# Four pairs of PSUM banks for a convolution, whole-batch-pair Fourier sums, and convolution units joined without emptying the array

## The chip, the cores and the metric

One NeuronCore of a Trainium2 chip runs the kernel. The metric is device time in microseconds of one execution. Everything below is about one core; TensorE is called PE, VectorE DVE, ScalarE ACT, GpSimd POOL and SyncE SP, as in the profile.

## The reference

A causal convolution over 3264 positions with 7 softmaxed taps per head (8 heads of 24 channels), then a Fourier layer: the first 64 modes of each channel are mixed by a 192 x 192 complex matrix per mode, transformed back and added to the signal, and a ReLU branch is added.

```python
# x: (8, 3264, 192), weight: (8, 7)
w = softmax(weight)                                  # per head
x = einsum('hk,bskhg->bshg', w, windows_of_7(x))     # causal, zero-padded
X = rfft(x, axis=1)[:, :64]
Yr = Xr @ w_r - Xi @ w_i                             # per mode, 192 x 192
Yi = Xr @ w_i + Xi @ w_r
u = x + irfft(Y, n=3264)
out = u + maximum(u @ w_ch, 0)
```

## The kernel before

The whole signal is held on chip in `xall`, in bf16: two batches at a time form a pair `q` (3 to 0, in the order in which they are loaded), and a pair's positions are six blocks `b` (5 to 0) of 256 rows in each half of the sequence, and a rest. POOL issues all loads of x (line 194) in that order, then those of the mixing weights (line 329). The weights of the first eight groups of four modes go to places in `ct` that are empty then, those of the next four to `arena`, which the convolution's stage also uses, and the rest to `arena` again as groups are done. All engines run in the order in which the program text issues their instructions.

**Convolution.** The blocks are cut into six *units* (the list at line 57: pair, first block, number of blocks, whether the rest rows belong to it). For each unit, `conv_head` (line 369) is called for 8 heads. A head is four steps: two output banks `a` by two inputs `b`. A step has lower matmuls (array rows 0 to 63) and upper ones (rows 64 to 127), which accumulate into the same bank. The upper matmuls of a step are put off by three steps (`LAG`, line 356, the list `upper`), so that both halves of the array work; `flush()` (line 359, called at line 546 after each unit) issues what is still put off. After a head's last upper step two instructions, one for each bank, carry the result from PSUM back to `xall` as bf16 (lines 403 and 405), on DVE for heads 0, 4 and 7 (0 and 7 where three folds fall into the unit), on ACT for the others. The banks come from `next_banks` (line 334): a ring of seven. The eighth bank, `sums[0]`, accumulates the Fourier sums. `rows_ahead` (line 338) copies edge rows of a pair from the top block to the rest, at the start of the unit that holds the top block.

**Fourier sums.** `fold` (line 417) makes sum and difference of the two halves of a piece of a unit, on DVE, in one of three places of `arena` in turn; it is called after heads 1 and 5 (1, 3 and 5) for the pieces of the unit before. After the unit's `flush()`, `xtrans` (line 451) transposes the sums of a pair that is done, and `dft` (line 427) multiplies the folded pieces with the table, 64 columns wide for each of two halves. The last unit's pieces are not folded: their products take the whole array, with twice the passes.

**Transposed copies.** 42 *jobs* (`tjobs`, line 511) transpose `xall` and the tables into `ct` and `gtab`, a bank of up to eight 128 x 128 transposes and a copy on DVE or ACT each. Six are done after the first unit, four after the third (lines 555 to 557), the others between the convolution and the mix (line 523, `trans_banks`) and in the mix.

**Mix and output.** The loop at line 918 goes over 16 groups: `mix(g)` (12 products with the weights, line 586), one or two jobs, products that are made ahead, and from group 1 on the transposition of the results (line 614). After group 13 all jobs that are left are done (line 946). `keep_busy` (line 904) issues products whose result isn't used. The output stage (line 832, a planned order) does the transformation back, ReLU, the additions and the stores.

Of the kernel before, what the change touches and what calls it, by code (L numbers as in the profile page):

```python
# [19 lines left out]
def kernel(  # L20
# [37 lines left out]
             [(1, 4, 2, 0), (1, 2, 2, 0), (1, 1, 1, 0)], [(1, 0, 1, 1), (0, 4, 2, 0), (0, 3, 1, 0)],  # L58
             [(0, 1, 2, 0), (0, 0, 1, 1)]]
# [77 lines left out]
    def temp(n, dtype):  # L137
# [23 lines left out]
    sides = [arena[:, FB * i:FB * (i + 1)].rearrange("p (r b t i d) -> p r b t i d", r=2, b=2, t=2, i=2)  # L161
             for i in (2, 1, 0)]
    assert pos[0] <= NWA * WGB - FB and NWA * WGB == 3 * FB
# [17 lines left out]
    cz = hand_out("left", "cv", (1, 1, 1, 1))  # L181
    sums = hand_out("right", "sum", (1, 1))
    stacks["sum"] = stacks.pop("right")
    cz += hand_out("right", "cv", (1, 1)) + [sums[1]]
# [149 lines left out]
    def next_banks():  # L334
        rot[0] += 2
        return [cz[(rot[0] - 2 + i) % 7] for i in range(2)]

    def rows_ahead(q):

        k = 2 + 4 * (NBH - 1)  # L340
        z = next_banks()
        for i in range(2):
            for h in range(2):
                nc.tensor.matmul(z[i][64 * (1 - h):64 * (1 - h) + 64, 0:2 * D], ahead[64:P, :],
                                 xall[64:P, q, k + 2 * h + i, :, :].rearrange("p t d -> p (t d)"), start=True,
                                 stop=True, tile_position=(64, 64 * (1 - h)), skip_group_check=True)
            engine = nc.vector.tensor_copy if i else nc.scalar.copy
            for h in range(2):
                r = slice(64 * (1 - h), 64 * (1 - h) + R0)
                engine(out=xall[r, q, i, :, :].rearrange("p t d -> p (t d)"), in_=z[i][r, 0:2 * D])  # L350
# [18 lines left out]
    def conv_head(u, h, engine):  # L369
        z = next_banks()  # L370
# [11 lines left out]
        def put(src, dst, c, a, b, fa, fb, back=0, start=False, stop=False):  # L382
# [3 lines left out]
            return nc.tensor.matmul(z[a][64 * dst:64 * dst + 64, GRP * (fa - f0):GRP * (fb - f0)],  # L386
# [3 lines left out]
        def later(a, b, name):  # L390
# [7 lines left out]
            if a == 1 and b == 0:  # L398
                for v in range(2):
                    dst = cflat[:, f0 // 2:f1 // 2, v, :, cols]  # L400
                    srcv = z[v][:, 0:GRP * (f1 - f0)].rearrange("p (n i e) -> p n i e", i=2, e=GRP)
                    if engine == "v":
                        nc.vector.tensor_copy(out=dst, in_=srcv)  # L403
                    else:
                        nc.scalar.copy(out=dst, in_=srcv)  # L405
# [11 lines left out]
    def fold(q, b0, nb, rest):  # L417

        side[0] += 1
        cpm = sides[(side[0] - 1) % 3]  # L420
# [6 lines left out]
    def dft(q, b0, nb, rest, cpm):  # L427
        xp = sums[0][:, 0:2 * D]
        ops = []
        for t in range(2 * b0, 2 * (b0 + nb)):  # L430
            b, a = divmod(t, 2)
            if cpm is None:
                ops.append((ftab[:, t, :], call[:, q, 1 + 2 * b, a, :, :], slice(0, P)))
                ops.append((fneg[:, t, :], call[:, q, 2 + 2 * b, a, :, :], slice(0, P)))
            else:
                for r in range(2):
                    ops.append((ftab[:, t, :], cpm[:, r, b - b0, a, :, :], slice(64 * r, 64 * r + 64)))
        if rest:
            for a in range(2):
                for r in range(1 if cpm is None else 2):  # L440
                    ops.append((ftab[:, 2 * NBH + a, :], call[:, q, 0, a, :, :],
                                slice(0, P) if cpm is None else slice(64 * r, 64 * r + 64)))
        top = b0 + nb == NBH
        for k, (f, mv, sl) in enumerate(ops):
            nc.tensor.matmul(xp[sl, :], f[:, sl], mv, start=(top and k < 2),  # L445
                             stop=(rest == 1 and k >= len(ops) - 2), tile_position=(0, sl.start),
                             skip_group_check=True)
        if rest:
            nc.scalar.copy(out=xs[q % 2][:], in_=xp.rearrange("p (i d) -> p i d", i=2))

    def xtrans(q):
        z = next_banks()
        for i in range(2):
            tp = z[i][:, 0:3 * P].rearrange("p (j c) -> p j c", j=3)
# [6 lines left out]
        for i in range(2):  # L461
            b = 2 * (NQ - 1 - q) + i
            dst = xt[:, :, b:2 * B:B, 0:MODES]
            srcv = z[i][:, 0:3 * P].rearrange("p (j c m) -> p j c m", j=3, c=2)
# [64 lines left out]
    prev = []  # L529
    pend = []  # L530
    todo = []
    for k, u in enumerate(units):
        for q, b0, nb, rest in u:
            if b0 + nb == NBH:
                rows_ahead(q)
        if k == 0:
            table(0)
        at = (1, 3, 5) if len(prev) == 3 else (1, 5)
        for h in range(H):
            conv_head(u, h, "v" if h in ((0, 7) if len(prev) == 3 else (0, 4, 7)) else "a")  # L540
            if h in at and prev:
                piece = prev.pop(0)
                todo.append((*piece, fold(*piece)))
            if k in (0, 1) and h == 6:
                table(k + 1)
        flush()
        for q in pend:
            xtrans(q)
        pend = []
        while todo and not pend:  # L550
            d = todo.pop(0)
            dft(*d)
            if d[3]:
                pend.append(d[0])
        if k in (0, 2):
# [428 lines left out]
```

## Time and profile before

| | us |
|---|---|
| Median of 3 runs | 176.45 (176.34 to 177.8) |
| The profiled execution | 175.09 |
| Its span, first to last instruction | 173.3 |
| First x that the chain of waits meets, landing | 26.84 |
| First product of the mix (line 586) | 78.36 |
| Line 586's last group | 107.9 |

The first 27 us are loads of x and the making of tables and taps, with the first unit. Units two to six, the sums and 16 of the jobs lie between 27 and 78, the mix between 78 and 108, and the output stage behind. A row of a view gives the start, the length, the engine, the line, what the instruction writes and reads, and in brackets the idle time before it and who ended it.

### The profile page before, as it was taken

Reading aid. Unit: us, or ns where it says so; the run is one execution under the profiler, and the core shown is the slowest. Engines: PE = TensorE matmul, PEld = TensorE weight load, DVE = VectorE, ACT = ScalarE, POOL = GpSimd, SP = SyncE. Lnnn points to the kernel's source line nnn. Section 1 sums busy time; section 2 is a strip of 40 time slices with the busy share of each in tenths; the row PEclk is TensorE's granted clock in tenths of the full one; section 3 lists DMA queues with packets and bytes.
Section 4 is the critical chain, followed back from the end, with each engine's and each line's share of the span. In section 5 each row is a group of like instructions: output and inputs, shape, how many; then the busy total and the mean of one; then the engine's idle time right before and its main releaser. Section 6 shows DMA issues by size and latency. Waiting matters only on the chain.

```text
span 173.3 us, 6286 instructions
## 1 busy us (share of the span) xinstructions
PE 152.2 (88%) x2635; PEld 116.2 (67%) x2635; DVE 133.0 (77%) x274; ACT 118.6 (68%) x250; POOL 64.3 (37%) x108
## 2 busy tenths in 40 slices
PE   0207988999999798998999999999999999999990
PEld 0004576666656565676776776688999988999960
DVE  3995589988997969735565653499998999999990
ACT  6736865557883836636767565588889899898860
POOL 7987969767766753082005500510000000000000
PEclk9999999999999999999999999999999999999997
DMA  3999999999999999999997994479879999999996
GB/s 29 179 183 199 201 202 200 202 201 203 201 201 196 203 208 205 206 207 206 207 179 110 194 193 82 103 269 362 315 253 371 395 352 356 351 354 392 377 351 197
DMA packets 38336, 40.72 MB, mean 235 GB/s; under 512 B 3652, under 2 KB 38212, under 8 KB 38308
## 3 DMA queue, kind: packets, MB, share of 16 engines
q0 software_dynamic: 23088, 19.96, 72.5%
q1 hardware_dynamic: 14948, 20.16, 32.4%
q8 instruction: 20, 0.33, 0.7%
q10 hardware_dynamic: 272, 0.20, 0.3%
q14 instruction: 8, 0.07, 0.1%
HBM read 39.43 MB, written 20.45 MB: 345 GB/s over the span
## 4 chain that ended last, share of the span: by engine, by line
PE 72%; DMA 9%; DVE 7%; POOL 6%; ACT 2%; issue 2%; POOLq 0%; DVEq 0%
PE outleft L733 18%; DMA xall<-in_x_dram 9%; PE sumright L733 9%; PE cvleft L386 8%; PE mixright L733 7%; PE trleft L504 7%; PE sumright L445 6%; POOL xall L194 5%; DVE arena L423 4%; PE cvright L386 3%; PE sumright L586 3%; PE trleft L733 2%; ACT ct L475 2%; PE mixright L614 2%; PE sumright L386 2%
## 5 line engine op out<-in xcount | busy, mean ns | idle before, releaser
L733 PEld LDWEIGHTS <-ct 64*128 64x128 bf16 x624 | 41.0, 94 | 5.0 <-PE trleft L733 0.5
L733 PE MATMUL outleft<-mixa,gtab 64*128 64x384 bf16 x182 | 41.9, 323 | 0.1
L386 PEld LDWEIGHTS <-band 64*64 64x64 bf16 x832 | 26.2, 108 | 23.0 <-issue 9.3
L386 PE MATMUL cvleft<-xall,band 64*64 64x432 bf16 (+7 forms) x484 | 34.6, 328 | 7.3 <-DMA xall<-in_x_dram 6.2
L194 POOL DMA_DIRECT2D xall<-in_x_dram x48 | 34.7, 735 | 8.5 <-DMA xall<-in_x_dram 7.2
L733 PEld LDWEIGHTS <-gtab 64*128 64x128 bf16 x416 | 30.9, 94 | 2.8 <-PE outleft L733 1.1
L779 ACT ACTIVATE outleft<-outleft 128x384 f32<-128x384 f32 x53 | 24.5, 477 | 4.6 <-PE outleft L733 2.3
L733 PE MATMUL mixright<-mixa,gtab 64*128 64x384 bf16 x90 | 25.8, 323 | 0.0
L733 PE MATMUL sumright<-mixa,gtab 64*128 64x384 bf16 x92 | 25.8, 323 | 0.0
L733 PE MATMUL outleft<-wb,ct 64*128 64x192 bf16 x104 | 23.1, 243 | 0.0
L386 PE MATMUL cvright<-xall,band 64*64 64x432 bf16 (+8 forms) x234 | 21.8, 329 | 1.3 <-DVE xall L403 0.8
L733 PE MATMUL outleft<-wa,ct 64*128 64x192 bf16 x104 | 22.9, 243 | 0.0
L733 PE MATMUL outleft<-wc,ct 64*128 64x192 bf16 x104 | 21.7, 243 | 0.0
L477 DVE COPY ct<-trleft 128x1024 bf16<-128x1024 bf16 (+1 forms) x18 | 11.8, 668 | 11.5 <-PE trleft L504 9.7
L405 ACT CAST xall<-cvleft 128x432 bf16<-128x432 f32 (+3 forms) x32 | 14.6, 519 | 8.5 <-DMA xall<-in_x_dram 3.5
L504 PEld LDWEIGHTS <-xall 128*128 128x128 bf16 x312 | 17.7, 98 | 3.7 <-issue 1.0
L423 DVE TENSOR_TENSOR arena<-xall 128x1536 bf16<-128x1536 bf16 (+1 forms) x24 | 19.2, 851 | 0.0
L801 DVE TENSOR_TENSOR arena<-outleft,xall 128x384 f32<-128x384 f32 x27 | 14.4, 554 | 2.5 <-PE outleft L733 2.1
L504 PE MATMUL trleft<-ident,xall 128*128 128x128 bf16 x234 | 16.2, 220 | 0.0
L403 DVE CAST xall<-cvleft 128x432 bf16<-128x432 f32 (+2 forms) x24 | 13.6, 603 | 3.1 <-PE sumright L386 2.0
L475 ACT COPY ct<-trleft 128x1024 bf16<-128x1024 bf16 x12 | 12.2, 1013 | 3.6 <-PE trleft L504 3.5
L386 PE MATMUL sumright<-xall,band 64*64 64x432 bf16 (+8 forms) x114 | 14.4, 324 | 0.0
(168 smaller groups left out, 339.3 us busy)
## 6 DMA issues: line engine op xcount, KB each, us to landing
xall<-in_x_dram POOLq DMA_DIRECT2D x48, 192.0 KB, 7.6
out_dram<-arena SPq DMA_DIRECT2D x23, 384.0 KB, 3.9
out_dram<-xall SPq DMA_DIRECT2D x13, 384.0 KB, 4.2
out_dram<-ct SPq DMA_DIRECT2D x8, 384.0 KB, 3.9
ct<-in_moe_w_r_dram POOLq DMA_DIRECT2D x8, 288.0 KB, 9.7
ct<-in_moe_w_i_dram POOLq DMA_DIRECT2D x8, 288.0 KB, 10.5
arena<-in_moe_w_r_dram POOLq DMA_DIRECT2D x8, 288.0 KB, 7.4
arena<-in_moe_w_i_dram POOLq DMA_DIRECT2D x8, 288.0 KB, 8.3
```

Source lines behind the costliest of these rows:

```text
L194: nc.gpsimd.dma_start(out=xall[:, q, k:k + 2, :, :].rearrange("p k t d -> p k (t d)"), in_=src)
L386: return nc.tensor.matmul(z[a][64 * dst:64 * dst + 64, GRP * (fa - f0):GRP * (fb - f0)], bd3[r, h, base:base + 64], xflat[r, fa - back:fb ...
L403: nc.vector.tensor_copy(out=dst, in_=srcv)
L405: nc.scalar.copy(out=dst, in_=srcv)
L423: nc.vector.tensor_tensor(out=cpm[:, r, 0:nb, :, :, :].rearrange("p b t i d -> p b (t i d)"), in0=src[:, :, 0, :], in1=src[:, :, 1, :], op=op)
L445: nc.tensor.matmul(xp[sl, :], f[:, sl], mv, start=(top and k < 2), stop=(rest == 1 and k >= len(ops) - 2), tile_position=(0, sl.start), sk ...
L475: nc.scalar.copy(out=out, in_=in_)
L477: nc.vector.tensor_copy(out=out, in_=in_)
L504: nc.tensor.transpose(o, cv.rearrange("p i d -> p (i d)")[:, P * blk:P * blk + P], ident[:])
L733: m = nc.tensor.matmul((Z[s % NZ] if bank is None else bank)[:, cols], l, r, start=start, stop=stop, skip_group_check=True)
L779: act = nc.scalar.activation(out=z, in_=z, func=ACT.Relu)
L801: add = nc.vector.tensor_tensor(out=o[:, :, a, :], in0=Z[s % NZ][:, 0:2 * D].rearrange("p (i d) -> p i d", i=2), in1=c_rows(q, kk)[:, a, : ...
```

## The change

All eight banks go to the convolution as four tiles of two banks. A head takes one tile (`next_pair`), and one instruction carries both banks out; DVE does heads 0 and 4 (0, 1, 3 and 5 of the first unit), ACT the others. `rows_ahead` uses one tile and two instructions of twice the length, and for the last two pairs is called after head 4 of the unit before. The units have four blocks each. Folds go to six places in turn, three in `arena` and three in `ct` of the second pair. `dft` is called once for a batch pair, with all its pieces, when its last piece has been folded, and accumulates in a tile of the same ring; `xtrans` of a pair comes just before the next pair's `dft`. `flush()` is called after the first and the last unit only, so that the put-off steps of the others run beneath the next unit's first head, behind whatever is issued between. After the third unit two jobs are done in place of four. The tables of `table(1)` and `table(2)` are made two units later. The mix takes four banks of its own, two of which first get a product each whose result isn't used.

```diff
     units = [[(3, 4, 2, 0), (3, 2, 2, 0)], [(3, 0, 2, 1), (2, 4, 2, 0)], [(2, 2, 2, 0), (2, 0, 2, 1)],
-             [(1, 4, 2, 0), (1, 2, 2, 0), (1, 1, 1, 0)], [(1, 0, 1, 1), (0, 4, 2, 0), (0, 3, 1, 0)],
-             [(0, 1, 2, 0), (0, 0, 1, 1)]]
+             [(1, 4, 2, 0), (1, 2, 2, 0)], [(1, 0, 2, 1), (0, 4, 2, 0)], [(0, 2, 2, 0), (0, 0, 2, 1)]]
...
     FB = 2 * 2 * 4 * D
-    sides = [arena[:, FB * i:FB * (i + 1)].rearrange("p (r b t i d) -> p r b t i d", r=2, b=2, t=2, i=2)
-             for i in (2, 1, 0)]
-    assert pos[0] <= NWA * WGB - FB and NWA * WGB == 3 * FB
+    sides = [a.rearrange("p (r b t i d) -> p r b t i d", r=2, b=2, t=2, i=2) for a in
+             [w[:, FB * i:FB * (i + 1)] for w, i in
+              ((ctw[1], 0), (ctw[1], 1), (arena, 2), (arena, 1), (arena, 0), (ctw[1], 2))]]
+    assert pos[0] <= NWA * WGB - FB and NWA * WGB == 3 * FB <= 3 * NT * P
...
-    cz = hand_out("left", "cv", (1, 1, 1, 1))
-    sums = hand_out("right", "sum", (1, 1))
-    stacks["sum"] = stacks.pop("right")
-    cz += hand_out("right", "cv", (1, 1)) + [sums[1]]
+    cz = hand_out("left", "cv", (2, 2)) + hand_out("right", "cv", (2, 2))
...
-    def next_banks():
-        rot[0] += 2
-        return [cz[(rot[0] - 2 + i) % 7] for i in range(2)]
+    def next_pair():
+        rot[0] += 1
+        return cz[(rot[0] - 1) % 4]
...
         k = 2 + 4 * (NBH - 1)
-        z = next_banks()
+        z = next_pair()
         for i in range(2):
             for h in range(2):
-                nc.tensor.matmul(z[i][64 * (1 - h):64 * (1 - h) + 64, 0:2 * D], ahead[64:P, :],
+                nc.tensor.matmul(z[64 * (1 - h):64 * (1 - h) + 64, i, 0:2 * D], ahead[64:P, :],
                                  xall[64:P, q, k + 2 * h + i, :, :].rearrange("p t d -> p (t d)"), start=True,
                                  stop=True, tile_position=(64, 64 * (1 - h)), skip_group_check=True)
-            engine = nc.vector.tensor_copy if i else nc.scalar.copy
-            for h in range(2):
-                r = slice(64 * (1 - h), 64 * (1 - h) + R0)
-                engine(out=xall[r, q, i, :, :].rearrange("p t d -> p (t d)"), in_=z[i][r, 0:2 * D])
+        for h, engine in enumerate((nc.scalar.copy, nc.vector.tensor_copy)):
+            r = slice(64 * (1 - h), 64 * (1 - h) + R0)
+            engine(out=xall[r, q, 0:2, :, :].rearrange("p i t d -> p i (t d)"), in_=z[r, :, 0:2 * D])
...
     def conv_head(u, h, engine):
-        z = next_banks()
+        z = next_pair()
         f0, f1 = extent(u)
         cols = slice(GRP * h, GRP * h + GRP)
...
             base = c + (0 if a == b else PB - 1 + a)
-            return nc.tensor.matmul(z[a][64 * dst:64 * dst + 64, GRP * (fa - f0):GRP * (fb - f0)],
+            return nc.tensor.matmul(z[64 * dst:64 * dst + 64, a, GRP * (fa - f0):GRP * (fb - f0)],
                                     bd3[r, h, base:base + 64], xflat[r, fa - back:fb - back, b, cols], start=start,
                                     stop=stop, tile_position=(64 * src, 64 * dst), skip_group_check=True)
...
             if a == 1 and b == 0:
-                for v in range(2):
-                    dst = cflat[:, f0 // 2:f1 // 2, v, :, cols]
-                    srcv = z[v][:, 0:GRP * (f1 - f0)].rearrange("p (n i e) -> p n i e", i=2, e=GRP)
-                    if engine == "v":
-                        nc.vector.tensor_copy(out=dst, in_=srcv)
-                    else:
-                        nc.scalar.copy(out=dst, in_=srcv)
+                dst = cflat[:, f0 // 2:f1 // 2, :, :, cols].rearrange("p n t i e -> p t n i e")
+                srcv = z[:, :, 0:GRP * (f1 - f0)].rearrange("p t (n i e) -> p t n i e", i=2, e=GRP)
+                if engine == "v":
+                    nc.vector.tensor_copy(out=dst, in_=srcv)
+                else:
+                    nc.scalar.copy(out=dst, in_=srcv)
...
         side[0] += 1
-        cpm = sides[(side[0] - 1) % 3]
+        cpm = sides[(side[0] - 1) % 6]
         src = call[:, q, 1 + 2 * b0:1 + 2 * (b0 + nb), :, :, :].rearrange("p (b h) t i d -> p b h (t i d)", h=2)
         for r, op in ((0, ALU.add), (1, ALU.subtract)):
             nc.vector.tensor_tensor(out=cpm[:, r, 0:nb, :, :, :].rearrange("p b t i d -> p b (t i d)"),
                                     in0=src[:, :, 0, :], in1=src[:, :, 1, :], op=op)
         return cpm
-    def dft(q, b0, nb, rest, cpm):
-        xp = sums[0][:, 0:2 * D]
+    def dft(q, parts):
+
+        xp = next_pair()[:, 0, 0:2 * D]
         ops = []
-        for t in range(2 * b0, 2 * (b0 + nb)):
-            b, a = divmod(t, 2)
-            if cpm is None:
-                ops.append((ftab[:, t, :], call[:, q, 1 + 2 * b, a, :, :], slice(0, P)))
-                ops.append((fneg[:, t, :], call[:, q, 2 + 2 * b, a, :, :], slice(0, P)))
-            else:
-                for r in range(2):
-                    ops.append((ftab[:, t, :], cpm[:, r, b - b0, a, :, :], slice(64 * r, 64 * r + 64)))
-        if rest:
-            for a in range(2):
-                for r in range(1 if cpm is None else 2):
-                    ops.append((ftab[:, 2 * NBH + a, :], call[:, q, 0, a, :, :],
-                                slice(0, P) if cpm is None else slice(64 * r, 64 * r + 64)))
-        top = b0 + nb == NBH
+        whole = slice(0, P)
+        for b0, nb, cpm in parts:
+            for t in range(2 * b0, 2 * (b0 + nb)):
+                b, a = divmod(t, 2)
+                if cpm is None:
+                    ops.append((ftab[:, t, :], call[:, q, 1 + 2 * b, a, :, :], whole))
+                    ops.append((fneg[:, t, :], call[:, q, 2 + 2 * b, a, :, :], whole))
+                else:
+                    for r in range(2):
+                        ops.append((ftab[:, t, :], cpm[:, r, b - b0, a, :, :], slice(64 * r, 64 * r + 64)))
+        for a in range(2):
+            for sl in [whole] if parts[-1][2] is None else [slice(64 * r, 64 * r + 64) for r in range(2)]:
+                ops.append((ftab[:, 2 * NBH + a, :], call[:, q, 0, a, :, :], sl))
         for k, (f, mv, sl) in enumerate(ops):
-            nc.tensor.matmul(xp[sl, :], f[:, sl], mv, start=(top and k < 2),
-                             stop=(rest == 1 and k >= len(ops) - 2), tile_position=(0, sl.start),
-                             skip_group_check=True)
-        if rest:
-            nc.scalar.copy(out=xs[q % 2][:], in_=xp.rearrange("p (i d) -> p i d", i=2))
+            nc.tensor.matmul(xp[sl, :], f[:, sl], mv, start=k < 2, stop=k >= len(ops) - 2,
+                             tile_position=(0, sl.start), skip_group_check=True)
+        nc.scalar.copy(out=xs[q % 2][:], in_=xp.rearrange("p (i d) -> p i d", i=2))
     def xtrans(q):
-        z = next_banks()
+        z = next_pair()
         for i in range(2):
-            tp = z[i][:, 0:3 * P].rearrange("p (j c) -> p j c", j=3)
+            tp = z[:, i, 0:3 * P].rearrange("p (j c) -> p j c", j=3)
             xsv = xs[q % 2][:, i, :].rearrange("k (p j) -> k j p", j=3)
             for j in range(3):
                 nc.tensor.matmul(tp[0:64, j, :], xsv[:, j, :], order[:], start=True, stop=True,
...
             dst = xt[:, :, b:2 * B:B, 0:MODES]
-            srcv = z[i][:, 0:3 * P].rearrange("p (j c m) -> p j c m", j=3, c=2)
+            srcv = z[:, i, 0:3 * P].rearrange("p (j c m) -> p j c m", j=3, c=2)
             if i == 0:
                 nc.vector.tensor_copy(out=dst, in_=srcv)
             else:
...
     prev = []
+    parts = {q: [] for q in range(NQ)}
     pend = []
-    todo = []
     for k, u in enumerate(units):
-        for q, b0, nb, rest in u:
-            if b0 + nb == NBH:
-                rows_ahead(q)
+        if k < 2:
+            rows_ahead(u[-1][0] if k else NQ - 1)
         if k == 0:
             table(0)
-        at = (1, 3, 5) if len(prev) == 3 else (1, 5)
+        done = None
         for h in range(H):
-            conv_head(u, h, "v" if h in ((0, 7) if len(prev) == 3 else (0, 4, 7)) else "a")
-            if h in at and prev:
-                piece = prev.pop(0)
-                todo.append((*piece, fold(*piece)))
-            if k in (0, 1) and h == 6:
-                table(k + 1)
-        flush()
-        for q in pend:
-            xtrans(q)
-        pend = []
-        while todo and not pend:
-            d = todo.pop(0)
-            dft(*d)
-            if d[3]:
-                pend.append(d[0])
-        if k in (0, 2):
-            for _ in range(3 if k == 0 else 2):
-                some(next_banks())
+            conv_head(u, h, "v" if h in ((0, 1, 3, 5) if k == 0 else (0, 4)) else "a")
+            if h in (1, 5) and prev:
+                q, b0, nb, rest = prev.pop(0)
+                parts[q].append((b0, nb, fold(q, b0, nb, rest)))
+                if rest:
+                    done = q
+            if h == 4 and k in (2, 3):
+                rows_ahead(units[k + 1][-1][0])
+            if h == 6 and k in (2, 3):
+                table(k - 1)
+        if k in (0, len(units) - 1):
+            flush()
+        if pend and done is not None:
+            xtrans(pend.pop())
+        if done is not None:
+            dft(done, parts[done])
+            pend.append(done)
+        for _ in range({0: 3, 2: 1}.get(k, 0)):
+            z = next_pair()
+            some([z[:, 0, :], z[:, 1, :]])
         prev = list(u)
     lt += hand_out("left", "tr", (1, 1, 1, 1))
     for g in range(NWC):
         load_w(g)
     trans_banks(2)
-    rot[0] = 4
-    for q in pend:
-        xtrans(q)
-    for d in todo:
-        dft(*d)
+    rot[0] = 2
+    xtrans(pend.pop())
+    dft(0, parts[0] + [(b0, nb, None) for q, b0, nb, rest in prev])
     for g in range(NWC, NWC + NWA):
         load_w(g)
-    for piece in prev:
-        dft(*piece, None)
     trans_banks(2)
-    rot[0] = 4
+    rot[0] = 2
     xtrans(0)
-    ye = hand_out("right", "mix", (1, 1))
+    sums = hand_out("right", "mix", (1, 1, 1, 1))
+    sums, ye = sums[0:2], sums[2:4]
+
+    for bank in sums:
+        nc.tensor.matmul(bank[:, 0:2 * D], ident[:], call[:, 0, 0, 0, :, :], start=True, stop=True, skip_group_check=True)
     trans_banks(2)
...
     second_stage()
-    for side in ("right", "sum", "left"):
+    for side in ("right", "left"):
         stacks[side].close()
```

## The prediction

> **What bounds the kernel now.** I read the page first, then the busy times by stage, then the chain of waits in order of time.
>
> ```profile
> span 173.3 us, 6286 instructions
> PEclk9999999999999999999999999999999999999997
> PE 72%; DMA 9%; DVE 7%; POOL 6%; ACT 2%; issue 2%; POOLq 0%; DVEq 0%
> ```
> ```profile
> 26.90:78.36 51.46, 49.59 (x939) 33.42 (x939) 42.68 (x72) 31.40 (x67) 32.50 (x50) 1.00 1.27 203
> 78.36:108.00 29.64, 28.79 (x517) 20.89 (x521) 16.08 (x32) 19.39 (x36) 6.10 (x10) 1.00 1.01 169
> ```
> ```profile
> 18.84 8.00 DMA xall<-in_x_dram
> ...
> 26.89 0.27 PE cvright L386
> ...
> 55.66 1.04 DVE xall L403 x2
> 56.70 3.47 DVE arena L423 x4
> ...
> 72.63 3.36 PE sumright L445 x26
> ...
> 77.35 1.00 PE trleft L504 x16
> 78.36 0.46 PE sumright L586 x11
> ```
>
> The columns of a stage are its length, then PE, weight load, DVE, ACT and POOL busy. Until 26.9 us the chain waits for x. From there to the first product of the mode mix (78.36) stands the stretch that the change rewrites: PE is busy 49.6 of 51.5 us at the full clock, so it is bound by TensorE and by the few places where DVE holds it. Between 78.4 and 108 PE is busy 28.8 of 29.6 us. So what the convolution wins arrives at the end, provided that the mix does not take it back; and a transposition moved from the first stretch to the second is not free.
>
> **What a unit costs.**
>
> ```profile
> 27.47 1.14 PE L386 MATMUL cvleft<-xall,band 64*64 64x432 bf16 x25
> ...
> 30.02 1.14 PE L386 MATMUL cvleft<-xall,band 64*64 64x432 bf16 x25
> ...
> 32.26 0.55 PE L386 MATMUL sumright<-xall,band 64*64 64x192 bf16 x6
> 32.74 1.65 PE L445 MATMUL sumright<-arena,ftab 128*64 128x384 bf16 x16
> 34.32 1.71 PE L386 MATMUL cvleft<-xall,band 64*64 64x432 bf16 x26
> ```
> ```profile
> 28.48 1.79 ACT L405 CAST xall<-cvleft 128x432 bf16<-128x432 f32 x4 [1.78 <-PE cvleft L386]
> 30.12 0.99 ACT L405 CAST xall<-cvright 128x432 bf16<-128x432 f32 x2
> ...
> 42.79 1.01 ACT L475 COPY ct<-cvleft 128x1024 bf16<-128x1024 bf16 x1
> 43.70 1.02 ACT L475 COPY ct<-cvright 128x1024 bf16<-128x1024 bf16 x1
> ```
> ```profile
> 38.82 1.12 DVE L403 CAST xall<-cvleft 128x432 bf16<-128x432 f32 x2
> 39.85 1.82 DVE L423 TENSOR_TENSOR arena<-xall 128x1536 bf16<-128x1536 bf16 x2
> 41.59 1.12 DVE L403 CAST xall<-cvleft 128x432 bf16<-128x432 f32 x2
> ```
>
> The first two PE rows are the same place of the ring of seven banks, 3.5 heads apart: 2.55/3.5 = 0.73 us a head of 432 columns, so 0.65 for 384. Of a head's four steps the upper rows run three steps late, beneath the next head; emptying them costs 3 x 0.73/4 = 0.55 us. ACT takes a head's two banks in (30.12 - 28.48)/2 = 0.82 us. One instruction of 864 elements has no row; from 0.41 us a start at 432 and 0.91 at 1024 I read 0.77 busy, some 0.9 until the result is there. DVE takes two banks in 39.85 - 38.82 = 1.03 and a fold (sum and difference) in 41.59 - 39.85 = 1.74; one instruction for two banks I put at 1.0. Two of them end 1.12 after the first starts, so joining them can hardly win more than 0.1; above, a pattern with one dimension more could cost more, which no row shows: that is a rival.
>
> On that the Trainium skill (Perfetto Trace Analysis, Optimizing Scalar/DVE Operations) has two rules. A PSUM access costs about 51 ns extra per ACT instruction and 125 ns per DVE one: ACT's rows agree (0.41 - 432 x 0.5/592 = 0.045), and a pair on DVE would then take 0.9, which shortens each DVE wait below by some 0.2 and the sum by about 0.4. The other speaks against the change: where an unsaturated engine makes bubbles elsewhere, instructions should be broken up, not joined.
>
> **Part by part.** Where x has landed:
>
> ```profile
> 33.03 0.71 POOL L194 DMA_DIRECT2D xall<-in_x_dram  x1 [0.26 <-DMA xall<-in_x_dram]
> ...
> 42.81 0.71 POOL L194 DMA_DIRECT2D xall<-in_x_dram  x1 [0.27 <-DMA xall<-in_x_dram]
> ```
> ```profile
> xall<-in_x_dram POOLq DMA_DIRECT2D x48, 192.0 KB, 7.6
> ```
>
> Loads are issued about 0.98 us apart and land after 7.6, so some eight are under way, and an issue that waits for a landing follows the load eight before it. The 32nd and 42nd issues put the 24th and 34th landings at about 32.75 and 42.5. Those close the third and the fourth unit of the new list (each reads one block below itself); the fifth and sixth have theirs long before.
>
> I walk the new order from 26.89, when the second unit starts in both kernels.
> - Second unit: no emptying, lower steps done at 32.3 (the rows show 32.74 with it). But the third waits for x until 32.75, so this joint earns only the moved sums behind it: the 16 products at 32.74 are gone from here.
> - Third unit: 8 x 0.73, and 0.32 for the edge rows, which now stand after head 4. DVE holds in this order head 0 (to 35.2), a fold (36.9), the edge-row copy (768 elements in one instruction, 0.9: 37.8) and head 4 (38.9). Head 7 needs head 4's pair at 38.2 and waits 0.7. End 39.6.
> - All 28 products of batches 6 and 7 in one go. The chain has one such go:
>
> ```profile
> 51.72 2.27 PE sumright L445 x28
> ```
>
>   0.081 each, 2.3: 41.9. One pair of transposition banks (16 matmuls, 1.0 by the row at 77.35, 0.9 without its tail): 42.8; x is there.
> - Fourth unit, 384 columns. Head 7 of the unit before still owes three upper steps; they run beneath head 0, then ACT needs 0.9, and head 1 uses that very pair, because one pair for the sums, one for the transpositions and one for head 0 lie between. PE waits 1.0. Then as above head 7 waits 0.9 for head 4. 8 x 0.65 + 0.32 + 1.9: 50.2. Before, the emptied array cost 0.55 here and the evacuation ran beneath the sums: at joints with sums the new order loses about 0.4.
> - Transposition of the sums 0.4 and 28 products: 52.9. Fifth unit with 0.8 for head 1: 59.6. Sixth joined without a gap, then emptied: 66.0. Here DVE has 2 x 1.0 + 2 x 1.74 = 5.5 us in a unit of 5.84, and just keeps up. With six places for the folds none waits for its readers.
> - 0.4, 28 products, 14 transposes, 0.4: 69.8. The last sums: one folded piece (8 x 0.081) and four blocks plus two rest rows unfolded. The row at 72.63 is 12 folded and 14 whole products in 3.36, so a whole one costs (3.36 - 0.97)/14 = 0.17, and the new set 0.65 + 18 x 0.17 = 3.7 against 3.4. With two banks: 74.4, and 74.8 after the last transposition of sums.
> - Its copies:
>
> ```profile
> 76.81 0.26 PE L457 MATMUL cvright<-loose 128*64 128x128 bf16 x1
> ...
> 77.22 0.56 DVE L466 CAST mixa<-cvright 128x384 bf16<-128x384 f32 x1
> 77.28 1.07 PE L504 MATMUL trleft<-ident,xall 128*128 128x128 bf16 x16
> ...
> 77.83 0.49 ACT L468 CAST mixa<-cvright 128x384 bf16<-128x384 f32 x1
> ```
>
>   DVE, then ACT, 1.2 to 1.4 us from the last matmul. Before, 16 transposes ran beneath them. The new order puts two filling products first, into the banks that these copies read, so PE waits about 1.3, then 0.33, then the transposes: first mix product at 77.3.
>
> The same walk over the order before (emptying at each unit, sums after it, waits of 1.1 and 0.95 for DVE in its last two units) passes 34.6, 43.7, 54.3, 64.1, 70.8 and ends at 77.9; the trace has 34.32 for the first and 78.36 for the end. The walk is half a us short, so I use the difference: **0.6 to 0.7 us earlier**.
>
> Against that, 8 transposition banks are done in the convolution instead of 10. The two left over go to the end of the mix:
>
> ```profile
> 104.18 0.50 PE L504 MATMUL trleft<-ident,xall 128*128 128x128 bf16 x6
> ...
> 104.93 0.47 PE L586 MATMUL sumright<-arena,mixa 128*16 128x192 bf16 x12
> ```
>
> Where 6 transposes stand, 22 will: 0.9 to 1.0 on a PE that has no idle time around it. Net **+0.3 us**. The weights allow it either way: loads of the last groups are released by the mix four groups earlier and move with it.
>
> ```profile
> 98.93 0.62 POOL L329 DMA_DIRECT2D arena<-in_moe_w_i_dram  x1
> ```
> ```profile
> arena<-in_moe_w_i_dram POOLq DMA_DIRECT2D x8, 288.0 KB, 8.3
> ```
>
> That lands near 107.2, and the last group's product starts after 107.9: an earlier mix has under a us there, unless its loads start earlier too. Three of the six places lie outside the arena, so the first of these loads no longer waits for the last fold; nobody waits for that.
>
> One more rule: the Trainium skill (TensorEngine Tiling, Key Properties) says that a change of tiling mode drains the array. By it the two joints that lose their sums would save four drains; the rows show the first sum at 32.74 while the convolution's rows run to 32.81, and the next unit at 34.32 before the sums' end at 34.39, so I count nothing. A drain of one pass (0.17, a whole product) each would take 0.6 off: 176.2, no other verdict.
>
> The profiled execution took 175.09 with a span of 173.3; the median of the runs is 176.45, 1.36 above it. 175.09 + 0.3 + 1.36 = **176.8**.
>
> **Rivals.** *The joints come for free (faster).* If evacuations keep ahead, the waits of 0.7, 1.0, 0.9 and 0.8 vanish: 3.4 less, 173.4; half of them, 175.1. For it: ACT has 6 x 0.77 = 4.6 us of work in 5.84. Against: it isn't a matter of load; head 1 and head 7 wait for one named instruction each. Chance over 1% faster: 0.18.
>
> *DVE or ACT becomes the bound (slower).* The pair instruction has a fourth free dimension in runs of 24. From 1.17 us a pair, DVE's 2 pairs and 2 folds exceed 5.84, and PE follows DVE through the two joined last units. At 1.3 times my price the same walk ends 1.8 later (178.6), at 1.5 times 4.5 later (181.3). Against: DVE's and ACT's rows already walk such runs, at about 1 ns an element. Together with a longer wait at the filling products (DVE's copy queued behind something), chance over 1% slower: 0.2.
>
> *It does less than it says:* the gain stays, and the 22 transposes fill gaps: 176.45 - 0.7 = 175.75, or the gain is eaten and 177.5. Both are no change.
>
> **How the numbers follow.** About 1% (1.8 us) is what a measurement here can tell from no change. My sum and its neighbours (175.1 to 177.9) hold 0.62. The range adds the faster rival to a little past its half and the slower one to its first price: 174.8 to 178.8.
>
> **What would show it.** In the changed profile: units starting near 32.8, 42.8, 52.9 and 59.6; PE waiting once or twice on ACT's evacuation (about 1.0 each) and on DVE's (0.7 to 0.9) in the third to fifth unit; a gap of over 1 us on PE before the filling products; the first mix product near 77.7; ACT's pair near 0.88 and DVE's near 1.05 us. I am wrong if a pair costs over 1.2, if the waits at heads 1 and 7 are missing, or if the mix, whose order is nearly unchanged, takes more or less than 30.6 us to 108.3.

## The result: 5% slower, nearly all of it before the mix

The changed kernel takes 185.97 us (median of 4 runs, 185.30 to 186.02) against 176.81 (4 runs) for the kernel before on the same chip: a ratio of 1.0502, 95% interval 1.0447 to 1.0557. Forecast were 176.8 us and "no change"; the range ended at 178.8. The profiled execution took 185.94. The profile before is one of 175.09, 1.7 under its median, so the two profiles differ by 10.85 where the medians differ by 9.2. In the runs further down, executions that were disturbed (the profiled one of e1, one of f3's ten, three of e4's four) are left out of the ratios, and e4, with one of 183.76 us left, has none.

The page of the changed kernel, from its head, the clock and the costliest groups:

```profile
span 184.0 us, 6219 instructions
...
PEclk9999999999969999999999999999999999999995
...
L400 ACT CAST xall<-cvleft 128x864 bf16<-128x864 f32 (+1 forms) x17 | 14.3, 863 | 9.9 <-PE cvleft L382 9.2
```

The span grew by 10.7 us. The joined evacuation costs what was forecast (863 ns is the mean of two sizes; one of 864 elements takes 0.88 us on ACT, a row below), so the instruction itself is not the loss. Busy times by stage, from the second unit's first product to the mix, through the mix, and in the one slice in which the clock digit is 6:

```profile
28.86:88.56 59.70, 51.41 (x939) 35.24 (x938) 36.27 (x47) 34.12 (x44) 32.02 (x49) 0.97 1.22 196
88.56:118.90 30.34, 29.73 (x544) 22.00 (x543) 16.88 (x33) 20.63 (x37) 4.93 (x8) 1.00 0.68 113
50.63:54.04 3.41, 3.41 (x49) 2.56 (x45) 2.62 (x3) 0.86 (x2) 1.81 (x4) 0.50 1.31 202
```

The mix starts at 88.56 instead of 78.36, 10.2 later, and is itself only 0.35 longer (30.34 against 29.99 from the first product to the end of the last group). The 10.2 are 1.96 by which the second unit starts later (28.86 against 26.90) and 8.24 by which the stretch from there is longer (59.70 against 51.46). In that stretch PE is busy 51.41 instead of 49.59, and idle 8.29 instead of 1.87. Most of the extra busy time is the third row: for 3.41 us the granted clock was 0.50, which costs up to 1.7. The idle time is what the change brought, 6.4 us of it. What ended PE's idle times between 14 and 90 us (in total, how often, longest; the row above these is the first unit's wait for x):

```profile
...
PE cvleft L382 <- DVE xall L398: 3.5, 2, 1.8
PE cvright L497 <- DVE ct L470: 1.6, 2, 0.9
PE cvleft L382 <- ACT xall L400: 1.4, 2, 0.8
PE mixright L569 <- ACT mixa L461: 1.2, 1, 1.2
PE cvright L497 <- ACT ct L468: 1.1, 1, 1.1
PE cvleft L497 <- DVE ct L470: 0.9, 1, 0.9
PE trleft L497 <- ACT loose L442: 0.6, 1, 0.6
...
```

The third and fourth rows are waits that the prediction had, at about their size. The fifth, the sixth and the second are transposition jobs (L497) that wait for the copy of another job: these it did not have. PE at the first joint, where three pairs of jobs stand, and below it the copies of DVE:

```profile
23.09 0.62 PE L497 MATMUL cvleft<-ident,xall 128*128 128x128 bf16 x8
24.57 0.61 PE L497 MATMUL cvleft<-ident,xall 128*128 128x128 bf16 x8 [0.85 <-DVE ct L470]
25.01 0.61 PE L497 MATMUL cvright<-ident,xall 128*128 128x128 bf16 x8
26.40 1.05 PE L497 MATMUL cvright<-ident,xall 128*128 128x128 bf16 x16 [0.78 <-DVE ct L470]
28.30 0.61 PE L497 MATMUL cvright<-ident,xall 128*128 128x128 bf16 x8 [0.85 <-DVE ct L470]
```
```profile
23.82 0.69 DVE L470 COPY ct<-cvleft 128x1024 bf16<-128x1024 bf16 x1 [0.96 <-PE cvleft L497]
25.66 0.69 DVE L470 COPY ct<-cvright 128x1024 bf16<-128x1024 bf16 x1 [1.14 <-PE cvright L497]
27.56 0.69 DVE L470 COPY ct<-cvright 128x1024 bf16<-128x1024 bf16 x1 [1.21 <-PE cvright L497]
```

The two jobs of a pair lie in the two banks of one tile. The first eight transposes end at 23.71, DVE copies their bank from 23.82 to 24.51, and only then, at 24.57, do the next eight begin, though they write the other bank. The program makes the second job's writes wait for the first job's read; that this is because both touch the same tile is what the experiments below test. Two readers of a tile follow each other in the same way. ACT and DVE around the edge rows (L346) of the third unit:

```profile
40.33 0.79 ACT L346 CAST xall<-cvright 16x768 bf16<-16x768 f32 x1
...
41.14 0.88 ACT L400 CAST xall<-cvright 128x864 bf16<-128x864 f32 x1
41.15 0.94 DVE L346 CAST xall<-cvright 16x768 bf16<-16x768 f32 x1 [1.27 <-ACT xall L346]
42.02 1.03 DVE L398 CAST xall<-cvleft 128x864 bf16<-128x864 f32 x1
...
43.11 0.98 PE L382 MATMUL cvleft<-xall,band 64*64 64x432 bf16 x16 [1.78 <-DVE xall L398]
```

DVE's copy starts 0.03 after ACT's ends. These two read both banks of the tile, each its own partitions, and so could also wait for a bank. The transposed sums (`xtrans`) separate the two: there DVE reads the first bank and ACT the second. The change, then e3, in which each bank is a tile of its own:

```profile
81.08 0.55 DVE L459 CAST mixa<-cvright 128x384 bf16<-128x384 f32 x1
81.67 0.48 ACT L461 CAST mixa<-cvright 128x384 bf16<-128x384 f32 x1 [0.39 <-DVE mixa L459]
```
```profile
71.97 0.55 DVE L461 CAST mixa<-cvright 128x384 bf16<-128x384 f32 x1
72.06 0.48 ACT L463 CAST mixa<-cvright 128x384 bf16<-128x384 f32 x1
```

On one tile ACT stands idle until DVE is through (81.63), though it reads another bank; on two tiles the copies overlap.

At the edge rows, head 4's evacuation stands behind DVE's copy in DVE's queue, and behind that PE, which needs its banks for head 7: 1.78 idle here, and 1.74 at the same place of the fourth unit.

### The profile page after: what moved, and what is told of

It is laid out like the page before. It is cut to its first block, busy times and chain, and to the rows that moved or that the text cites. A ratio compares the mean times of both kernels' runs of the same rounds, so it can differ in the third digit from the quotient of the medians.

```text
span 184.0 us, 6219 instructions
## 1 busy us (share of the span) xinstructions
PE 154.7 (84%) x2637; PEld 119.0 (65%) x2637; DVE 125.8 (68%) x244; ACT 120.6 (66%) x220; POOL 64.3 (35%) x108
## 4 chain that ended last, share of the span: by engine, by line
PE 69%; DMA 12%; POOL 6%; ACT 6%; DVE 3%; issue 2%; POOLq 0%; DVEq 0%
PE outleft L727 17%; PE mixright L727 15%; DMA xall<-in_x_dram 12%; PE cvleft L382 7%; PE trleft L497 7%; PE cvright L382 6%; POOL xall L191 5%; PE cvright L440 5%; PE mixright L580 3%; ACT ct L468 2%; PE trleft L727 2%; PE mixright L608 1%; ACT xall L400 1%; PE cvleft L440 1%; DVE xall L795 1%
## 5 line engine op out<-in xcount | busy, mean ns | idle before, releaser
L382 PEld LDWEIGHTS <-band 64*64 64x64 bf16 x832 | 28.1, 112 | 26.0 <-issue 13.8
L382 PE MATMUL cvleft<-xall,band 64*64 64x432 bf16 (+4 forms) x432 | 34.1, 342 | 10.6 <-DMA xall<-in_x_dram 5.7
L727 PE MATMUL mixright<-mixa,gtab 64*128 64x384 bf16 x182 | 41.0, 323 | 0.0
L382 PE MATMUL cvright<-xall,band 64*64 64x432 bf16 (+4 forms) x400 | 31.2, 348 | 0.4 <-issue 0.4
L773 ACT ACTIVATE mixright<-mixright 128x384 f32<-128x384 f32 x51 | 23.7, 478 | 3.2 <-PE mixright L727 1.0
L497 PEld LDWEIGHTS <-xall 128*128 128x128 bf16 x312 | 18.0, 98 | 7.6 <-issue 4.9
L400 ACT CAST xall<-cvleft 128x864 bf16<-128x864 f32 (+1 forms) x17 | 14.3, 863 | 9.9 <-PE cvleft L382 9.2
L400 ACT CAST xall<-cvright 128x864 bf16<-128x864 f32 (+1 forms) x17 | 14.3, 855 | 9.7 <-PE cvright L382 4.6
L727 PE MATMUL mixright<-wa,ct 64*128 64x192 bf16 x84 | 19.5, 243 | 0.0
L727 PE MATMUL mixright<-wb,ct 64*128 64x192 bf16 x84 | 19.3, 243 | 0.0
L727 PE MATMUL mixright<-wc,ct 64*128 64x192 bf16 x84 | 17.8, 243 | 0.0
L497 PE MATMUL trleft<-ident,xall 128*128 128x128 bf16 x248 | 16.9, 220 | 0.6 <-ACT loose L442 0.6
## 6 DMA issues: line engine op xcount, KB each, us to landing
ct<-in_moe_w_i_dram POOLq DMA_DIRECT2D x8, 288.0 KB, 10.2
```

What stands on the lines that cost most here:

```text
L382: return nc.tensor.matmul(z[64 * dst:64 * dst + 64, a, GRP * (fa - f0):GRP * (fb - f0)], bd3[r, h, base:base + 64], xflat[r, fa - back:fb ...
L497: nc.tensor.transpose(o, cv.rearrange("p i d -> p (i d)")[:, P * blk:P * blk + P], ident[:])
L727: m = nc.tensor.matmul((Z[s % NZ] if bank is None else bank)[:, cols], l, r, start=start, stop=stop, skip_group_check=True)
L773: act = nc.scalar.activation(out=z, in_=z, func=ACT.Relu)
```

## The experiments

The kernel before ran beside each group of experiments (e, f and g; medians 176.71, 176.53 and 176.55), so their times can be set against each other. Two theories stood against each other. *The tile is the unit of waiting*: what was a wait between banks before is now a wait between halves of a tile. *The joints*: four of the six units are no longer emptied, and heads 1 and 7 meet evacuations that are late, as the prediction had it, only more so.

| Kernel | Median, us | Ratio to the kernel before (95%) |
|---|---|---|
| the change | 185.97 | 1.0502 (1.0447 to 1.0557) |
| e1: first joint's jobs in own tiles | 182.55 | 1.0342 (1.0295 to 1.0389) |
| e2: edge rows on ACT alone | 181.15 | 1.0272 (1.0215 to 1.0329) |
| e3: eight single banks | 178.39 | 1.0109 (1.0064 to 1.0154) |
| e4: fillers in the other banks | 187.13 | not readable |
| f1: e1 and e2 | 179.27 | 1.0168 (1.0130 to 1.0205) |
| f3: f1, joints emptied | 178.58 | 1.0106 (1.0066 to 1.0145) |
| f4: e3, e2's rows, e4 | 176.76 | 1.0018 (0.9982 to 1.0054) |
| f5: f4, joints emptied | 175.79 | 0.9971 (0.9945 to 0.9996) |
| g1: f3, all jobs in own tiles | 177.52 | 1.0055 (1.0024 to 1.0086) |
| g3: g1, fillers later | 175.77 | 0.9973 (0.9947 to 0.9999) |
| g2: f5, fillers later | **173.98** | **0.9874 (0.9841 to 0.9907)** |
| g4: g2, ten jobs in the convolution | 176.44 | 0.9997 (0.9964 to 1.0030) |

**e1, the second job of each pair at the first joint in a tile of its own.**

```diff
-            some([z[:, 0, :], z[:, 1, :]])
+            some([z[:, 0, :], (next_pair()[:, 0, :] if k == 0 else z[:, 1, :])])
```

> The changed kernel, but each of the six transposition jobs behind the first unit takes a tile of its own. Theory A (an access to one bank of a two-bank tile waits for the access to its other bank): the three waits of PE on a DVE copy there, 0.85 + 0.78 + 0.85 in the changed kernel's profile, go, the second unit starts some 2.5 us earlier, and the time falls from 186.0 to about 183.5. Rival B (the first unit is late because the PE clock came up at 19.9 us there and 17.5 us before, and the joints cost the rest): the second unit comes less than 1 us earlier, 185 or more.

Measured: 182.55, 3.4 below the change, more than expected. The order of the work, its amount and the instructions are the same; only the tile of three jobs differs, and with it the place in the ring of what follows. The profile of f1, which holds this edit, shows the same 48 transposes:

```profile
23.27 0.62 PE L497 MATMUL cvleft<-ident,xall 128*128 128x128 bf16 x8
24.29 1.07 PE L497 MATMUL cvright<-ident,xall 128*128 128x128 bf16 x16 [0.39 <-ACT xall L400]
25.19 1.06 PE L497 MATMUL cvleft<-ident,xall 128*128 128x128 bf16 x16
26.08 0.61 PE L497 MATMUL cvright<-ident,xall 128*128 128x128 bf16 x8
```

No job waits for another's copy; the one wait is for a head's evacuation, and the whole takes 3.42 instead of 5.82 us. Nor is it the first unit that makes the second late, as the rival had it: in the change the first joint is reached at 23.09, in the kernel before at 21.73, but f1 reaches it at 23.27 and starts the second unit with its edge rows at 26.62, where the change does at 28.84.

**e2, both edge-row copies on ACT.** They read the same tile either way and follow each other either way; what differs is that DVE's queue is free.

```diff
-        for h, engine in enumerate((nc.scalar.copy, nc.vector.tensor_copy)):
+        for h, engine in enumerate((nc.scalar.copy, nc.scalar.copy)):
```

> The changed kernel, but ACT makes both copies of the edge rows, DVE none. Theory A: DVE's copy stood behind ACT's copy of the same tile, and head 4's evacuation behind it, so PE's waits on DVE before head 7 of the third and fourth unit (1.78 and 1.74 us) fall under 0.7 each; about 183.8. Rival C: ACT then is late with heads 5 and 6 by its second copy of 0.8 us, PE waits on ACT instead, and the time stays within 1 us of 186.0.

Measured: 181.15, 4.8 below, twice what was expected. Its list of PE's waits:

```profile
PE cvright L497 <- DVE ct L470: 1.6, 2, 0.8
PE cvleft L382 <- ACT xall L400: 1.4, 2, 0.8
PE mixright L569 <- ACT mixa L461: 1.2, 1, 1.2
PE cvright L497 <- ACT ct L468: 1.1, 1, 1.1
PE cvleft L497 <- DVE ct L470: 0.8, 1, 0.8
...
```

The row of 3.5 us is gone, not shortened: what PE met there was the queue behind the edge rows, not an evacuation that is late by itself. Every other wait of the change's list behind the first unit has stayed. The clock never falls in this profile, so part of what exceeds 3.5 may be the clock's; that was not separated.

**e3, eight tiles of one bank.** The ring, the order and the places in PSUM are those of the change; a head's evacuation is two instructions again, and the edge rows are split by bank again.

```diff
-    cz = hand_out("left", "cv", (2, 2)) + hand_out("right", "cv", (2, 2))
+    cz = hand_out("left", "cv", (1, 1, 1, 1)) + hand_out("right", "cv", (1, 1, 1, 1))
...
-        return cz[(rot[0] - 1) % 4]
+        return [cz[(2 * (rot[0] - 1) + i) % 8] for i in range(2)]
```

> The changed kernel in its order, units, folds and joints, but with eight tiles of one bank: a head takes two of them in turn and each bank has its own evacuation, as before. Theory A: the job waits and the edge-row waits both go, and PE's second wait at the jobs behind the third unit (1.1 us); 2.5 + 2.2 + 1.1 us less, about 180.2. Rival C (the late evacuation at the joints and the two jobs moved are what costs): 184 or more.

Measured: 178.39, 7.6 of the 9.2 us that the change lost, and more than expected (its profile is of a faster execution, 176.21). The 48 transposes of the first joint, and PE's waits (three rows of them):

```profile
21.92 0.98 PE L499 MATMUL cvleft<-ident,xall 128*128 128x128 bf16 x9
23.06 0.56 PE L499 MATMUL cvleft<-ident,xall 128*128 128x128 bf16 x7 [0.15 <-ACT xall L402]
23.46 1.95 PE L499 MATMUL cvright<-ident,xall 128*128 128x128 bf16 x32
```
```profile
...
PE cvleft L383 <- DVE xall L400: 1.2, 2, 0.7
PE mixright L571 <- ACT mixa L463: 1.0, 1, 1.0
PE cvleft L383 <- ACT xall L402: 0.8, 2, 0.4
...
```

From first to last the transposes take 3.49 instead of 5.82 us. No job waits for another's copy; the waits at the edge rows are 1.2 instead of 3.5 and those at the joints 0.8 instead of 1.4. A reason that fits, not tested by itself, is that PE can start on the first bank of a head before the second is out. So joining the two evacuations earned nothing that outweighs what the wider tile costs.

**e4, the fillers into the other two banks of the mix's pool**, which the last transposed batch did not use.

```diff
-    sums, ye = sums[0:2], sums[2:4]
+    sums, ye = sums[2:4], sums[0:2]
```

> The changed kernel, but the mix's first two banks are the pair that the last sums left, not the pair that the last transposition of sums wrote, so the two filling products don't wait for its copies. Theory: PE's wait of 1.2 us before the fillers goes and 16 transposes cover the copies again: 184.8. Rival: the first mix product waits for the same copies anyway, and nothing is won.

The times don't settle it. The same edit is in f4 and f5, and there the fillers wait 1.0 us, as they do in e3 without it. On single banks, at least, this expectation fell. The likely reason, not tested by itself, is that a new pool's tile waits for the readers of the whole pool that it replaces, not for those of its own bank.

**f1, e1 and e2 together.** 

> The changed kernel with both repairs: jobs behind the first unit in tiles of their own, edge rows by ACT alone; heads still leave a two-bank tile by one instruction. If the two waits are separate they add: 186.0 - 3.4 - 4.8 = 177.8, close to the eight single banks (178.4), and the single evacuation itself costs nothing. If the joined evacuation of a pair costs by itself, 180 or more.

Measured: 179.27. The two gains do not add (3.4 and 4.8 alone, 6.7 together). The fall of the clock, up to 1.7, may be in both of them; no run separates that.

**f3 and f5, the array emptied at the joints with sums, on two-bank tiles and on single banks; f4, e3 with the edge rows on ACT and e4's edit.**

```diff
-        if k in (0, len(units) - 1):
+        if k not in (1, 4):
             flush()
```

> The kernel with both repairs, and the array emptied also at the two joints where sums are made (after the third and fourth unit). My prediction's step: a joint with sums loses 0.4 us by being joined, so this wins 0.8 in all: about 177.0 if the other is 177.8. Rival, as the change means it: an emptying costs 0.55 each and joining is a win, so this is about 1 us slower.

> The eight single banks with edge rows by ACT alone and the filling products on the banks of the last sums. In the profile of the eight single banks PE waits 0.49 and 0.70 us on DVE in the third and fourth unit and 1.01 before the fillers: 178.4 - 2.2 = 176.2, the time of before or a little under. Rival: the 1.01 comes back at the first mix product, 177.2.

> The same with the array emptied at the two joints with sums. With one evacuation per bank PE's waits on ACT at the joints are 0.43 and 0.34 in the eight single banks, less than the 0.79 and 0.66 with pairs, so emptying should win nothing here: within 0.5 us of the kernel without it. If the step of 0.4 a joint holds for single banks too, 0.8 less.

Measured: 178.58 (0.7 below f1), 176.76, and 175.79 (1.0 below f4). Emptying the array at the two joints with sums is 0.35 to 0.5 cheaper for each than leaving it full (the executions of one kernel scatter by 1.4 to 2.4 us here, so this is rough). That is the prediction's "about 0.4" by which the new order loses there; on single banks it had been expected to vanish, and did not. The joint theory is right in kind, then, and accounts for about a tenth of the loss. The two joints without sums were not tested.

**g1, the third joint's jobs in tiles of their own too.** 

> The kernel with the first joint's three jobs in tiles of their own, the edge rows' copies all on ScalarE and the array emptied at the joints (178.6 us), with one edit more: the third joint's two jobs also write tiles of their own. Theory of the tile as the unit of waiting: the wait of 1.10 us of the second job's transposes behind the first job's copy goes, about 177.5 us. Rival (the wait is of the bank rings, any later use of the ring meets it): no change, 178.6 us.

Measured: 177.52, 1.06 below f3, as the theory of the tile has it. PE's waits on copies are down to the fillers, the last sums and two short ones:

```profile
...
PE mixright L569 <- ACT mixa L461: 1.2, 1, 1.2
PE trleft L497 <- ACT loose L442: 0.6, 1, 0.6
PE mixright L608 <- ACT band L591: 0.5, 1, 0.5
PE cvright L497 <- ACT xall L400: 0.4, 1, 0.4
```

**g2 and g3, the fillers behind the 16 transposes of the next two jobs**, on f5 and on g1.

```diff
+    trans_banks(2)
     for bank in sums:
         nc.tensor.matmul(bank[:, 0:2 * D], ident[:], call[:, 0, 0, 0, :, :], start=True, stop=True, skip_group_check=True)
-    trans_banks(2)
```

> The kernel with eight single banks, edge rows on ScalarE and emptied joints (175.8 us), with the two filler products behind the 16 transposes of the next two jobs instead of ahead of them. The fillers wait about 1.0 us for copies of the last transposed batch; the 16 transposes take about 1.2 us and don't need those banks. Theory (the wait is hidden by the transposes): about 174.8 us, below the kernel before the change (176.8 us) by 1%. Rival (the transposes' own banks are not free yet, so that the wait only moves): 175.8 us.

> Both edits on the two-bank tiles: jobs of all joints in tiles of their own and the fillers behind the 16 transposes. If each wait goes by itself: 1.1 us and about 1.0 to 1.2 us below 178.6 us, about 176.4 us. If the fillers' wait only moves: 177.5 us.

Measured: 173.98 and 175.77, each some 1.8 below the kernel without the edit. PE around the fillers (L572) in g2:

```profile
75.87 1.07 PE L499 MATMUL trleft<-ident,xall 128*128 128x128 bf16 x16
76.95 0.48 PE L572 MATMUL mixright<-xall,ident 128*128 128x384 bf16 x2
77.37 0.46 PE L582 MATMUL mixright<-ct,mixa 128*16 128x192 bf16 x12
```

The copies run beneath the transposes and the fillers wait for nothing. The gain is more than the wait: the mix's second group is shorter too (1.43 to the next group instead of 1.80 in the change), since the wait of 0.5 on L608, in g1's rows above, has no counterpart here. g2 beats both kernels, by 1.3% the one before. g3, the kernel with the same repairs on two-bank tiles, is still 1.8 behind g2, so even with its waits taken out the wider tile does not pay. Where these 1.8 us lie was not traced.

**g4, two of the jobs moved back from the mix's end to the third joint.** 

> The single-bank kernel with fillers moved, with ten jobs of the transposed table in the convolution instead of eight (two more at the third joint), so that two fewer stand at the mix's end. If a job costs the same in either place: within 0.3 us of the kernel with eight. If the jobs at the mix's end were hidden: about 0.9 us slower (two times eight transposes at the joint). If they stand exposed there and are cheaper at the joint: up to 0.5 us faster.

Measured: 176.44, 2.5 above g2, beyond all that was expected. The mix of g2 and then of g4:

```profile
77.37:107.33 29.96, 29.71 (x543) 22.01 (x543) 16.42 (x32) 20.21 (x37) 6.37 (x11) 1.00 1.03 172
```
```profile
79.49:109.50 30.01, 29.16 (x527) 21.10 (x527) 15.64 (x31) 19.01 (x35) 5.50 (x9) 1.00 0.97 161
```

PE is busy 0.55 less with two jobs fewer, but the mix is no shorter. Its fourteenth group is 0.89 shorter (2.44 to the next one instead of 3.33), but the second and the sixth are longer (1.89 and 2.03 instead of 1.43 and 1.50), as they are in the kernel before, which also does ten jobs in the convolution (1.89 and 2.03). The mix starts 2.1 later. Of that, 1.1 is there before the joint (in the first unit, where both programs are the same, PE's products behind the last wait for data start at 16.22 instead of 15.12), and about 1.0 is the 16 transposes. So moving two jobs out of the convolution is worth about 1.0 us in these profiles, because it costs nothing in the mix; what makes up the rest of the 2.5 stays open.

## Why the prediction was wrong

The walk through the stages, and what the traces have at its points:

| Step | Forecast | Measured |
|---|---|---|
| second unit starts | 26.89 | 28.86 |
| head 7 of the third unit waits | 0.7 | 1.78 |
| a pair of jobs at the third joint | 0.9 to 1.0 | 2.3 (46.41 to 48.67) |
| head 1 behind the third joint waits | 1.0 | 0.79 |
| head 7 of the fourth unit waits | 0.9 | 1.74 |
| head 1 behind the fourth joint waits | 0.8 | 0.66 |
| fillers wait | 1.3 | 1.23 |
| evacuation of a pair, ACT and DVE | 0.88, 1.05 | 0.88, 1.03 |
| two jobs more at the mix's end | 0.9 to 1.0 | 0.35 over the mix |

**The step that failed** is "I walk the new order from 26.89, when the second unit starts in both kernels", and with it "One pair of transposition banks (16 matmuls, 1.0 by the row at 77.35, 0.9 without its tail)". The first takes the six jobs at the first joint to cost what they cost before, and the second prices two jobs by a row in which sixteen transposes go to two *tiles* of one bank. In the changed kernel they go to two halves of one tile, where the second job waits for the first one's copy: 0.85, 0.78 and 0.85 at the first joint and 1.10 at the third, 3.6 us in all. The 48 transposes of the first joint take 5.82 us; in the kernel before they took 3.67 (21.73 to 25.40). Part of the first 2.5 had been slack before, when PE waited for x until 26.89. The pair at the third joint, in the changed kernel (the last row is the next unit):

```profile
46.41 0.62 PE L497 MATMUL cvright<-ident,xall 128*128 128x128 bf16 x8
...
48.13 0.61 PE L497 MATMUL cvright<-ident,xall 128*128 128x128 bf16 x8 [1.10 <-ACT ct L468]
48.67 0.93 PE L382 MATMUL cvleft<-xall,band 64*64 64x384 bf16 x16
```

**The same omission once more** stands in the walk of DVE through the third unit ("the edge-row copy (768 elements in one instruction, 0.9: 37.8) and head 4 (38.9)"). The duration is right (0.94), but the copy was taken to start when DVE is free. It starts when ACT's copy of the same tile is over, which adds 1.1 and 0.8 to the two waits at head 7.

**The sum does not close.** The walk puts the first mix product at 77.3, and it came at 88.56, 11.3 later. Of that, 2.0 are the late second unit, 1.4 the pair at the third joint, 1.9 the waits at head 7, up to 1.7 the half clock, and 1.0 two waits that the walk does not have (0.57 before the transposes at 79.56, 0.42 at 70.00); the waits that came out shorter than forecast give back 0.4. The other 3.7 or more lie in units that took longer than heads at 0.73 and 0.65 would: the last two, from 61.92 to 76.17, took 14.25 instead of 13.1. Why, no run shows.

**What held.** The price of the joined evacuation (on DVE 1.03, and not the 0.9 that the prediction weighs beside its own figure), so the rival in which DVE or ACT becomes the bound by a dearer instruction is not what happened; the waits at head 1; the loss of 0.4 at a joint; the wait of the fillers. The two jobs cost 0.90 at the mix's end (3.33 from the start of the fourteenth group to that of the next, instead of 2.43), as forecast, but the sixth group has become 0.53 shorter (1.50 for 2.03), so the term was 0.35 over the mix, oversized by 0.6; g4 shows that the sixth group goes with the number of jobs.

**No rival named it.** The slower rival had the right sign and a wrong mechanism. That the change could make work wait that did not wait before was considered for engines and queues, and not for the tiles themselves, although the diff shows them grow from one bank to two.

What the half clock cost is not settled: four executions of the change at mean clocks from 0.979 to 0.993 differ by 0.7 us at most, so it is not the main part.

## What to carry to other kernels

When buffers are merged, list everything that used to go to one of them, by any engine, and check each pair of uses that now shares a tile: here a waiting pair cost 0.8 to 1.1 us each time, against 0.06 saved by joining two evacuations on ACT (0.88 us for one of two banks; two single ones in e3 are through 0.94 after the first starts). Take the price of a step only from a row in which it has the same tiles, not just the same instructions. And a wait that stands ahead of independent work can be bought off by order alone: moving two products behind sixteen transposes was worth 1.8 us.

## What the runs showed of the hardware

The granted clock of TensorE fell to 0.50 for 3.41 us (50.63 to 54.04) in the change's profile, with no idle stretch of PE longer than 1.78 us since the second unit began, but with three of them, 3.7 us in all (1.78, 1.10 and 0.79), in the 9.3 us ahead. In the profiles of e2, e3 and f1 to g4, which lack one or more of these waits, it did not fall there. The Trainium skill (TensorE: Matmul & The Clock Gate, section "A second HAM failure mode: psum-queue depth-cycling") tells of a kernel in which PE idles briefly between groups of matmuls so often that the clock oscillates. This trace has one such fall, behind three short waits, and no oscillation, so it fits without showing that rule. That the waits caused the fall was not tested by itself.
